# A new order for every queue of a fused attention and gated-convolution kernel, with 139 elementwise steps on another engine

## The chip, the cores and the metric

The kernel runs on one core of one Trainium2 chip. A core has TensorE (PE in the profile) for matrix products, three elementwise engines, VectorE (DVE), ScalarE (ACT) and GpSimd (POOL), and SyncE (SP), which here only issues DMAs. Each engine takes its instructions strictly from its own list; engines wait for each other by semaphores. TensorE writes its products to PSUM, a small memory that VectorE and ScalarE read; everything else lies in SBUF. The metric is the time on the device in microseconds (us), the median of several runs. One further execution was taken with the hardware profiler; every row below is from it.

## The reference

Four batches, eight heads, 768 positions, head width 64, model width 512. Four of the eight heads are full causal ("retrieval"); the others see the first 4 positions and a window of 64. The attention's output, heads side by side, is the input of a gated long convolution.

```python
scores = scale * np.matmul(q, k.transpose(0, 1, 3, 2))
mask = np.where(retr[0, :, 0, 0, None, None], full_mask, stream_mask)
scores = np.where(mask[None, :, :, :], scores, -1000000000.0)
a = np.exp(scores - np.max(scores, axis=-1, keepdims=True))
attn = np.matmul(a / (np.sum(a, axis=-1, keepdims=True) + 1e-09), v)

proj = x @ w_proj
x1, x2, x3 = (proj[..., :D], proj[..., D:2 * D], proj[..., 2 * D:])
x2_conv = np.fft.irfft(np.fft.rfft(x2, n=S, axis=1) * H, n=S, axis=1)
y = x1 * x2_conv * x3
return (y @ w_out).astype(np.float32)
```

Here `x` is the attention's output with its heads side by side, and `H` the spectrum of `filter_fft` along the positions.

## The kernel before

A short opening issues the loads of q and k of the first two head pairs (k of pair 0, q of pair 0, k of pair 1, q of pair 1, in this order, on SyncE), makes a few constants and the first of three parts of a table of angles, and checks which heads are full. Then the function `patterned` does everything else. It defines 995 named steps, each a handful of instructions, and issues them in the order of a long string of words, `FAST`. That string is the whole schedule: since nothing reorders afterwards, the words that belong to one engine stand in that engine's list in the order of the string. A word is a step's name, with `@n` where the step opens one of four PSUM slots of two banks, and `/s`, `/v`, `/p` or `/d` where the engine may be chosen: ScalarE, VectorE, GpSimd or a DMA. Where a step needs another's result, or a buffer that another still reads, the program waits by a semaphore, and whatever is queued behind it on that engine waits too.

```python
    for word in FAST.split():
        name, _, slot = word.partition("@")
        name, _, eng = name.partition("/")
        now.update(slot=slot, engine=eng)
        ops[name]()
```

The steps, by the names that the text uses (n is one of 16 head pairs, b one of 4 batches):

- `lq`, `lk`, `lv`: loads of q, k, v of a pair. `cq`, `ck`, `cv` (from pair 8 on `cqk` for both): casts to bf16.
- `T`, `E`: transposes of q and k on TensorE and their eviction from PSUM; from pair 8 on `T` is a DMA transpose. `kx`, `ks`, `vx`, `vs`: small copies that put the first 4 positions beside the window's keys and values.
- `sc`, `sb`, `ex`, `mk`, `at`: score products, a bias added by a product with a table `btab`, exponentials on ScalarE, masks, product with v. `rec`, `nm`: the row sums' reciprocal and the division, from PSUM into `attn`.
- `fd`, `fe`, `fA`, `fS`, `fb`, `fr`: sums and differences of the attention's output that fold its 768 positions, ahead of the transform `W`, evicted by `We`.
- `angle`, `turns`, `wrap`, `size`, `sin`, `cos`: the table `G` of the transform, made by ScalarE's sine. `Gt`, `Ge`: its transpose. `lfilt`, `fold`, `F`, `H`: the filter's load, folding, transform and scaling.
- `X`, `Xe`, `pa`, `pb`, `pc`, `sw`: the projection of the spectrum, and its product with the filter's. `c`, `ce`, `cv` with three numbers: the inverse transform and the sum and difference of its halves. `x1`, `x3`, `xs`, `g`, `y`: the two gates. `tn`, `te`: transposes of the attention's output. `o`, `oe`, `st`: output product, eviction and store. `lw`, `lwo`: weight loads.
- `blank`: products of zeros whose result is not used, which keep TensorE at work.

The helper that carries most engine choices is at L1101 to L1110:

```python
    def ev(out, in_):
        if now["engine"] == "v":
            nc.vector.tensor_copy(out=out, in_=in_)
        elif now["engine"] == "p":
            nc.gpsimd.tensor_copy(out=out, in_=in_)
        elif now["engine"] == "d":
            nc.sync.dma_start(out=out, in_=in_)
        else:
            nc.scalar.copy(out=out, in_=in_)

    def two(out, a, b, op):
        (nc.gpsimd if now["engine"] == "p" else nc.vector).tensor_tensor(out, a, b, op)
```

The division `nm` has two forms: on VectorE one instruction for the whole pair, on ScalarE (`/s`) twelve, one for each block of 128 rows and head.

Of the kernel before, what the change touches and what calls it, by code (L numbers as in the profile page):

```python
# [144 lines left out]
at4.1@1 at4.0 rec4 nm4/v kx6/s vs5/s sc6.1@2 sc6.0@3 ex6.1 pb0.1/p ex6.0 cqk8/p T8 at5.1@0 at5.0 sc6.2@1 ex6.2 rec5
nm5/v fe5/v pa0.2/v T7.1@2 T7.0 E7.1/s pc0.1/v x10.0.1@3 E7.0/s x10.0.0 xs0.0/s x10.1.0@1 H2.4 kx7/v ks7/s mr6
mk6.2 x30.0.1@0 x30.0.0 g0.0 x10.1.1 sc7.1@2 fd5/v xs0.1/s ex7.1 fe4/p pb0.2/v pc0.2/v fA5/v mk7.1 pb0.0/v
x10.3.1@3 x10.3.0 lk9 lq9 lv7 sc7.2@0 sc6.4@1 pa0.0/v xs0.3/s ex6.4 lq10 ex7.2 mk7.2 x10.2.1@2 tn4@3 mk6.0 pc0.0/v
fS5/v mk6.1 fb5/p x10.2.0 c0.1.0@1 te4/s cv6/s xs0.2/s x30.2.0@0 vx6/p x30.2.1 vs6/s ce0.1/s lwo g0.2 sc7.0@3 ex7.0
# [10 lines left out]
o0.4.1 nm9/v fe9/v Xe1.2/s fd9/v oe0.5/s x31.0.0@3 fA9/v kx11/p sc10.2@0 ex10.2 pb1.1/v sc11.1@2 fS9/v sc11.2@1  # L160
ex11.2 lv11 x31.0.1 x11.3.1@0 g1.0 mk11.2 pa1.1/v mk10.2 mr10 x11.3.0 vx10/p ex11.1 mk11.1 cv11/s vx11/v xs1.3/s
fb8/v vs11/s X1.0.0@1 X1.0.1 Xe1.0/s at10.1@3 at10.0 st0.3 T12 fb9/p sc11.0@2 ex11.0 sc12.0@0 x11.2.0@1 fr8 x11.2.1
sw1.0 rec10 pc1.1/v nm10/v W8.0@2 ex12.0 sw1.1 pb1.2/v W8.1 st0.5 xs1.2/s x11.1.1@3 mk11.0 x11.1.0 We8/s fd10/v
xs1.1/s tn10@0 at11.1@1 at11.0 te10/s pa1.0/v lk13 tn9@2 te9/s fr9 W9.1@3 W9.0 x31.2.1@0 fe10/v rec11 nm11/v fe11/v
pa1.2/v sc12.4@2 sc12.1@1 x31.2.0 fA10/p pc1.2/v lq13 We9/s ex12.4 fd11/v x31.1.0@3 tn11@2 x31.1.1 ex12.1 g1.2
te11/s sc12.3@1 sc12.2@0 fS10/v x12.0.1@2 x12.0.0 ex12.2 sc12.5@0 g1.1 ex12.3 x32.0.1@3 xs2.0/s c1.1.0@1 lv12 lq14
lk14 fb10/v pb1.0/v pc1.0/v exp0 fr10 W10.1@2 ce1.1/s lq15 W10.0 We10/s ex12.5 x32.0.0 cqk14/s fA11/p fS11/v mk12.1
cqk13/v c1.1.1 fr11 fb11/v g2.0 c1.0.1@2 lv14 c1.0.0 cv1.1.0 lk15 cv14/s cv1.1.1 W11.0@0 W11.1 c1.3.0@3 We11/s
c1.3.1 mk12.2 ce1.0/v cv1.0.1 c1.2.1@1 cv1.0.0 mk12.0 c1.2.0 X2.0.1@0 ce1.3/s y1.1/p cv1.3.1 X2.0.0 y1.0/v cv1.3.0
X2.1.0@2 cv12/s T13 kx13/v ce1.2/s cv1.2.0 cv1.2.1 Xe2.0/s pa2.0/v ks13/p cqk15/s X2.1.1 sc13.0@3 sc13.2@1 ex13.2  # L170
pb2.0/v y1.3/v at12.1@0 vx14/d Xe2.1/s y1.2/v lv13 ex13.0 cv13/v T14 ks14/s at12.0 rec12 nm12/v kx14/s x31.3.1@1
T15 x31.3.0 o1.1.0@2 g1.3 fd12/v fe12/p vs13/d vx13/d fA12/v sc13.1@3 sc14.1@0 sc14.2@1 mk13.0 ex13.1 lv15 mk13.1
o1.1.1 o1.0.0 ex14.1 o1.0.1 mk13.2 X2.2.1@3 kx15/v oe1.1/s mk14.1 ex14.2 st1.1 X2.2.0 Xe2.2/s pa2.1/v at13.1@0
sw2.0 ks15/v pb2.1/v at13.0 rec13 sc14.0@2 ex14.0 sw2.1 sc15.2@1 x12.2.0@3 x12.2.1 xs2.2/s mk14.2 tn12 nm13/v
ex15.2 x32.2.1@2 x32.2.0 sc14.4@3 sc14.3@0 ex14.4 pc2.1/v cv15/s sc15.0@1 g2.2 pc2.0/v sc15.1@3 pa2.2/v o1.2.0@2
o1.3.0 o1.3.1 ex15.1 fS12/p ex15.0 fe13/p fb12/v fd13/p vs14/d o1.2.1 ex14.3 fr12 x12.1.1@3 x12.1.0 mk14.0 mr14
fA13/v mk15.0 at14.0@1 at14.1 pb2.2/v x32.1.0@0 oe1.3/s x12.3.0@2 xs2.1/s mk15.1 W12.0@3 x12.3.1 W12.1 rec14 nm14/v
vx15/s mk15.2 vs15/s at15.1@1 at15.0 xs2.3/s We12/s x32.1.1 pc2.2/v c2.0.1@2 tn13 c2.1.0@3 fS13/v c2.0.0 fr13
ce2.1/s fb13/p rec15 nm15/v g2.1 fe14/p fd15/v st1.3 fd14/p fS14/v W13.1@1 fA14/v fr14 W13.0 We13/s c2.1.1 fb14/p
cv2.1.0 cv2.1.1 ce2.0/s cv2.0.1 o1.5.0@0 o1.5.1 o1.4.0 cv2.0.0 o1.4.1 c2.3.0@1 fe15/p tn14 oe1.5/s st1.5 fA15/v  # L180
W14.0@3 W14.1 We14/s fS15/p fb15/v c2.3.1 fr15 c2.2.1@2 y2.0/v c2.2.0 y2.1/v W15.1@0 W15.0 ce2.3/s We15/s x32.3.1@3
ce2.2/s x32.3.0 cv2.3.0 cv2.3.1 y2.3/v g2.3 cv2.2.1 cv2.2.0 y2.2/v X3.1.0@0 X3.2.0@1 X3.2.1 Xe3.2/v sw3.0 X3.1.1
sw3.1 Xe3.1/s pa3.2/v o2.0.0@3 o2.0.1 o2.1.0 o2.1.1 pa3.1/v oe2.1/s pb3.1/p X3.0.0@2 o2.4.0@1 o2.4.1 tn15@0 te15/s
pb3.2/v X3.0.1 o2.5.0 o2.5.1 pc3.1/v x33.0.0@3 x13.0.1@0 st2.1 Xe3.0/s x13.1.0@2 pa3.0/v pc3.2/v x13.0.0 x13.1.1
# [1717 lines left out]
```

## Time and profile before

| what | value |
|---|---|
| median of 3 runs | 188.08 us (187.79 to 188.16) |
| profiled execution, its span from first to last instruction | 188.0 us |
| TensorE busy | 171.7 us, 91%, 1688 instructions |
| VectorE busy | 152.6 us, 81%, 301 instructions |
| ScalarE busy | 143.3 us, 76%, 191 instructions |
| GpSimd busy | 64.1 us, 34%, 96 instructions |
| DMA | 33.67 MB, mean 179 GB/s |
| mean granted TensorE clock | 0.997 |

The span of the profiled execution and the median of the runs agree within 0.1 us, so a time worked out from the span needs no correction that a run could tell. A busy time is the time in which an engine had an instruction in its datapath. The page of the profile also gives, for a group of equal instructions, their count, busy time, the mean of one, and the idle time of the engine just before them with what ended it.

### The profile page before, as it was taken

The numbers are of one execution on the slowest core, as the hardware profiler recorded it, in microseconds if no ns is written. First come the engines' busy times: TensorE is split into PE (matmuls) and PEld (weight loads), VectorE is DVE, ScalarE is ACT, GpSimd is POOL, SyncE is SP. The second block draws the span as 40 slices with busy tenths as digits, with TensorE's granted clock in tenths as the row PEclk, the third lists the DMA queues.
The fourth block names the chain that finished last, engine by engine and source line by source line (L and its number), as shares of the span: only waits on it lengthen the run. The fifth ranks groups of instructions, "written<-read, shape, count | busy, mean of one in ns | idle before, by whom it ended". The sixth has DMA issues, their size and how long they took to land.

```text
span 188.0 us, 4376 instructions
## 1 busy us (share of the span) xinstructions
PE 171.7 (91%) x1688; PEld 103.9 (55%) x1704; DVE 152.6 (81%) x301; ACT 143.3 (76%) x191; POOL 64.1 (34%) x96
## 2 busy tenths in 40 slices
PE   0889996989999999999999999999999999999960
PEld 0346773644585556565556656475567644565430
DVE  6559676968999998998799999999799996388720
ACT  6689995879997998987999999899895526613330
POOL 3368750992080094443210111311406405400200
PEclk9999999999999999999999999999999999999998
DMA  5999999699999899999899988688942205300363
GB/s 182 309 271 281 194 187 287 151 260 228 218 210 203 180 192 210 184 232 234 193 249 257 225 180 176 137 138 225 127 125 55 112 2 157 122 3 0 113 248 104
DMA packets 77695, 33.67 MB, mean 179 GB/s; under 512 B 66850, under 2 KB 74082, under 8 KB 77666
## 3 DMA queue, kind: packets, MB, share of 16 engines
q1 hardware_dynamic: 74576, 30.29, 70.4%
q0 software_dynamic: 2944, 2.88, 10.1%
q8 instruction: 15, 0.25, 0.6%
q10 hardware_dynamic: 146, 0.13, 0.2%
q14 instruction: 14, 0.11, 0.2%
HBM read 24.64 MB, written 6.29 MB: 165 GB/s over the span
## 4 chain that ended last, share of the span: by engine, by line
PE 65%; DVE 14%; DMA 7%; POOL 4%; ACT 3%; issue 2%; SPq 0%; POOLq 0%; DVEq 0%
PE f_x_ps L1695 18%; PE f_X_ps L1660 10%; PE f_out_ps L1758 8%; PE f_c_ps L1725 7%; PE f_sc L1492 6%; PE f_att L1556 6%; DMA qk_ahead<-in_q_dram 4%; DMA f_qk_f<-in_q_dram 3%; DVE f_attn L1573 2%; ACT f_pT L1511 2%; PE f_W_ps L1617 2%; DVE f_P L1110 2%; PE f_sc L1505 2%; DVE f_fo L1110 1%; DVE turns L1736 1%
## 5 line engine op out<-in xcount | busy, mean ns | idle before, releaser
L1511 ACT ACTIVATE f_pT<-f_sc 128x1024 bf16<-128x1024 f32 (+3 forms) x68 | 58.7, 918 | 3.7 <-PE f_sc L1492 3.2
L1695 PE MATMUL f_x_ps<-f_xT,f_wproj 128*128 128x384 bf16 x256 | 46.7, 326 | 0.4 <-DVE f_attn L1573 0.3
L1695 PEld LDWEIGHTS <-f_wproj 128*128 128x128 bf16 x256 | 23.9, 98 | 16.5 <-issue 1.6
L1660 PE MATMUL f_X_ps<-f_wproj,f_xh 128*128 128x512 bf16 x92 | 22.3, 379 | 0.2
L1758 PE MATMUL f_out_ps<-f_wout,f_gy 128*128 128x512 bf16 x86 | 21.7, 379 | 0.3
L1492 PE MATMUL f_sc<-f_qkT 64*128 64x128 bf16 (+3 forms) x248 | 20.3, 250 | 0.0
L1725 PE MATMUL f_c_ps<-f_Gi,f_P 128*128 128x384 bf16 x96 | 18.4, 326 | 0.2 <-DVE f_gy L1714 0.2
L1110 POOL TENSOR_TENSOR f_fo<-f_attn 128x384 bf16<-128x384 bf16 x13 | 12.3, 954 | 15.0 <-DVE f_attn L1573 14.8
L1736 DVE TENSOR_TENSOR turns<-angle,f_c_ps 128x384 bf16<-128x384 f32 x32 | 16.3, 548 | 1.3 <-PE f_c_ps L1725 0.8
L1556 PE MATMUL f_att<-f_v_aug,f_pT 128*128 128x65 bf16 x392 | 17.2, 193 | 0.0
L1556 PEld LDWEIGHTS <-f_pT 128*128 128x128 bf16 x472 | 16.0, 97 | 2.1 <-issue 0.4
L1107 ACT COPY f_o<-f_out_ps 128x1024 f32<-128x1024 f32 (+2 forms) x12 | 10.2, 854 | 8.7 <-PE f_out_ps L1758 7.8
L1573 DVE TENSOR_TENSOR f_attn<-f_att,f_rec 128x768 bf16<-128x768 f32 x16 | 15.3, 955 | 0.6
L1492 PEld LDWEIGHTS <-f_qkT 64*128 64x128 bf16 x248 | 10.6, 94 | 9.3 <-issue 7.0
L1660 PEld LDWEIGHTS <-f_xh 128*128 128x128 bf16 x96 | 9.0, 98 | 10.3 <-issue 0.7
L1107 ACT CAST f_xh<-f_W_ps 128x768 bf16<-128x768 f32 x13 | 10.5, 807 | 4.5 <-PE f_W_ps L1617 2.3
L1758 PEld LDWEIGHTS <-f_gy 128*128 128x128 bf16 x92 | 8.6, 98 | 9.3 <-DVE f_gy L1718 0.3
L1107 ACT CAST f_X<-f_X_ps 128x1024 bf16<-128x1024 f32 x10 | 10.2, 1016 | 4.6 <-PE f_X_ps L1660 4.5
L1531 DVE TENSOR_TENSOR f_pT<-f_pT,mtab 128x1024 bf16<-128x1024 bf16 (+1 forms) x18 | 12.1, 688 | 1.4 <-ACT f_pT L1511 1.4
L1447 PE MATMUL f_qkT_ps<-identity,f_qk_bf 128*128 128x128 bf16 x96 | 7.9, 225 | 5.6 <-DVE f_qk_bf L1101 5.2
L1725 PEld LDWEIGHTS <-f_P 128*128 128x128 bf16 x96 | 9.0, 98 | 6.5 <-issue 0.6
L1110 POOL TENSOR_TENSOR f_br<-f_fo,f_uv 128x256 bf16<-128x256 bf16 x6 | 4.6, 765 | 21.3 <-DVE f_uv L1110 12.3
(132 smaller groups left out, 329.9 us busy)
## 6 DMA issues: line engine op xcount, KB each, us to landing
f_v_f<-in_v_dram SPq DMA_DIRECT2D x32, 192.0 KB, 4.4
out_dram<-f_o SPq DMA_DIRECT2D x17, 256.0 KB, 2.3
qk_ahead<-in_k_dram SPq DMA_DIRECT2D x6, 384.0 KB, 6.3
qk_ahead<-in_q_dram SPq DMA_DIRECT2D x6, 384.0 KB, 6.3
qk_ahead<-in_k_dram SPq DMA_DIRECT2D x10, 192.0 KB, 4.3
qk_ahead<-in_q_dram SPq DMA_DIRECT2D x10, 192.0 KB, 4.9
f_wproj<-in_moe_w_proj_dram POOLq DMA_DIRECT2D x6, 256.0 KB, 7.2
out_dram<-f_o SPq DMA_DIRECT2D x3, 512.0 KB, 4.4
```

The costliest lines, as they stand in the source:

```text
L1107: nc.scalar.copy(out=out, in_=in_)
L1110: (nc.gpsimd if now["engine"] == "p" else nc.vector).tensor_tensor(out, a, b, op)
L1492: nc.tensor.matmul(sc[:, bank, col:col + 128 * cnt], lhsT=keys, rhs=qkT(n)[rows, 0, 128 * i:128 * (i + cnt)], start=(col == 0 or not biase ...
L1511: nc.scalar.activation(out=pT(n)[:, c, :, 0:w], in_=held[f"sc.{n}.{c}"][:, :, 0:w], func=AF.Exp, scale=SCALE)
L1531: nc.vector.tensor_mul(some, some, near(c)[:, None].to_broadcast([128, 2, cols, 128]))
L1556: nc.tensor.matmul(att[:, hh, 65 * i:65 * i + 65], lhsT=pT(n)[:, c, bank, col:col + 128], rhs=values, start=(z == 0), stop=(z == len(here) ...
L1573: nc.vector.tensor_mul(attn(n).rearrange("p i hh d -> p hh i d"), rows[:, :, :, 0:64], held[f"rec.{n}"][:, :, :, None].to_broadcast([128, ...
L1660: nc.tensor.matmul(ps[:, u, :], lhsT=xh(b)[:, cc, chain, 128 * part:128 * part + 128], rhs=wproj()[:, cc, DM:2 * DM], start=(cc == 0), sto ...
L1695: nc.tensor.matmul(ps[:, s, 0:HS], lhsT=wproj()[:, cc, part * DM + cb * 128:part * DM + (cb + 1) * 128], rhs=xT(b)[:, cc, s * HS:s * HS + HS],
L1725: nc.tensor.matmul(ps[:, r, 0:HS], lhsT=P(b)[:, t, u, ch], rhs=Gi()[:, tile_no], start=(m == 0), stop=(m == 2))
L1736: fn(conv[:, half * HS:half * HS + HS], held[f"evs.{b}.{cb}"], held[f"c_ps.{b}.{cb}"][:, 1, 0:HS])
L1758: nc.tensor.matmul(ps[:, i % 2, :], lhsT=gy(b)[:, cb, i * 128:(i + 1) * 128], rhs=wout()[:, cb, :], start=(cb == 0), stop=(cb == NC - 1))
```

## The change

The string `FAST` is written anew. The same 995 steps stand in it, in another order, and 139 of them name another engine. No instruction's shape changes but where the engine has its own form (`nm` on ScalarE). The opening's steps are as before.

```diff
 FAST = """
-angle1 turns1 angle2 ck1/p cq0/p turns2 lq2 ones0 ck0/v wrap1 T0.1@0 wrap2 blank0@1 wrap0 sin2 size E0.1/s sin1 lk2
-cq2/p kz2 cos2 cq1/s T0.0 E0.0/v lv1 lk3 lv0 T1.0@2 ones2 cos1 T2.0@3 E2.0/v sc0.3@1 E1.0/s T1.1 mtab2 E1.1/s
...
+cq1/s lv0 cq0/v angle2 turns1 T1.0@0 turns2 angle1 wrap0 ck0/s lq2 wrap1 wrap2 T0.0@1 T0.1 blank0@2 size ck1/s E0.0/v
+E0.1/v E1.0/v mtab2 mtab3 kz1 cos1 ones1 T1.1 cos2 btab lv1 lk2 ones0 sc0.2@3 E1.1/v sc0.3@1 lq3 sin1 sin2 sc0.1@2
...
```

By engine the 139 steps go like this. To GpSimd 55: 39 from VectorE (`fd` 5, `fe` 3, `fA` 4, `fS` 5, `fb` 3, `y` 4, `pa` 2, `pc` 2, casts 6, small copies 5), 13 from ScalarE (`cqk` 3, `cv` 5, small copies 5) and 3 small copies from a DMA. From GpSimd 30: 24 to VectorE (casts 7, folds 9, `pb` 2, `y` 1, small copies 5) and 6 to ScalarE. From VectorE to ScalarE 26, among them `nm5`, `nm14` and `nm15`; from ScalarE to VectorE 27, among them `E` 7, `ce` 4 and `te` 3; one small copy goes from a DMA to ScalarE.

Two places show the new order. The first is ScalarE's list in the opening, from its first steps in `patterned` to the first exponential (`f_pT<-f_sc`). `qk_ahead_68` is the buffer of pair 1's q and k, `qk_ahead_65` that of pair 0; `f_G` is the table of sines and cosines; an `ACT_TABLE_LOAD` stands where ScalarE goes over from sine to exponential. Before:

```order
L1192 ACTIVATE turns<-fcol,tfrac 128x384 x2
L1214 ACTIVATE f_G<-angle 128x3x2x64
L1107 COPY f_qkT_3005<-f_qkT_ps_2983 128x768
L1214 ACTIVATE f_G<-angle 128x3x2x128
L1214 ACTIVATE f_G<-f_size,quarter 128x3x2x64
L1107 CAST f_qk_bf_2972<-qk_ahead_68 128x768
L1214 ACTIVATE f_G<-f_size,quarter 128x3x2x128
L1107 COPY f_qkT_3051<-f_qkT_ps_3029 128x768 x2
L1511 ACT_TABLE_LOAD
L1511 ACTIVATE f_pT_3076<-f_sc_3_3048 128x2x384
```

After, on the same engine and at the same place:

```order
L1106 CAST f_qk_bf_2969<-qk_ahead_68 128x768
L1191 ACTIVATE turns<-fcol,tfrac 128x384 x2
L1106 CAST f_qk_bf_2974<-qk_ahead_65 128x768
L1106 CAST f_qk_bf_2969<-qk_ahead_68 128x768
L1213 ACTIVATE f_G<-f_size,quarter 128x3x2x128
L1213 ACTIVATE f_G<-f_size,quarter 128x3x2x64
L1213 ACTIVATE f_G<-angle 128x3x2x128
L1213 ACTIVATE f_G<-angle 128x3x2x64
L1510 ACT_TABLE_LOAD
L1510 ACTIVATE f_pT_3088<-f_sc_3_3053 128x2x384
```

The cast of pair 1's q (`cq1`) has moved from behind most of the table to the head of the list, the casts of both k (`ck0`, `ck1`) have come over from the other engines, and the three evictions (`COPY f_qkT`) have gone to VectorE. On TensorE the transposes follow in the order `T1.0`, `T0.0`, `T0.1`, eight blanks, `T1.1`, where it was `T0.1`, eight blanks, `T0.0`, `T1.0`, `T2.0`. (In the changed file every line behind the string has a number smaller by one.)

The second place is GpSimd's list, from its first step in `patterned` to the load of the filter (`f_filt`). `mtab` is the table of masks from which `btab` is made. Before:

```order
L1103 CAST f_qk_bf_2972<-qk_ahead_68 128x768
L1103 CAST f_qk_bf_2974<-qk_ahead_65 128x768
L1383 MEMSET f_v_aug_2979 128x12
L1103 CAST f_qk_bf_3009<-f_qk_f_2_2977 128x768
...
L1165 AFFINE_SELECT mtab<-mtab 128x3x128
...
L1103 COPY f_v_x_3100<-f_v_aug_3078 64x520
L1227 TENSOR_SCALAR f_G<-par 128x3
L1103 CAST f_v_aug_3036<-f_v_f_2_3089 128x12x64
L1103 COPY f_v_x_3164<-f_v_aug_3036 64x4x65
L1264 DMA f_filt<-in_moe_filter_fft_dram 128x6x512
```

After:

```order
L1164 AFFINE_SELECT mtab<-mtab 128x3x128
...
L1102 CAST f_v_aug_3047<-f_v_f_0_2971 128x12x64
L1226 TENSOR_SCALAR f_G<-par 128x3
L1102 CAST f_qk_bf_3091<-f_qk_f_2_2989 128x768
L1378 MEMSET f_kx_3135 128x4x64
L1102 COPY f_v_x_3140<-f_v_aug_3032 64x520
L1102 CAST f_qk_bf_3164<-qk_ahead_65 128x768
L1263 DMA f_filt<-in_moe_filter_fft_dram 128x6x512
```

The mask table has moved ahead of all casts, the three casts of q and k of pairs 0 to 2 have left, and ahead of the filter's load now stand a write into the table `G` (the step `alt`), the casts of k of pairs 2 and 3, and a copy of pair 1's v that waits for its cast (`cv1`) on VectorE.

The third place is SyncE's list of loads, behind the load of v of pair 3 (`f_v_f_3`). The buffers `qk_ahead_68` and `qk_ahead_65` take the loads of pairs 4 and 6 here, `f_qk_f_8` those of pair 8. Before:

```order
L1401 DMA f_qk_f_5_3156<-in_k_dram 128x2x384
L1404 DMA f_qk_f_8_3302<-in_k_dram 128x6x64 x2
L1401 DMA qk_ahead_68<-in_k_dram 128x2x384
L1401 DMA qk_ahead_68<-in_q_dram 128x2x384
L1401 DMA qk_ahead_65<-in_q_dram 128x2x384
```

After:

```order
L1422 DMA f_v_f_2_3167<-in_v_dram 128x6x64 x2
L1400 DMA f_qk_f_5_3230<-in_k_dram 128x2x384
L1400 DMA f_qk_f_5_3230<-in_q_dram 128x2x384
L1400 DMA qk_ahead_68<-in_k_dram 128x2x384
L1400 DMA qk_ahead_68<-in_q_dram 128x2x384
L1422 DMA f_v_f_5_3474<-in_v_dram 128x6x64 x2
```

The load of pair 8's k, whose buffer must first be free of pair 5's k, no longer stands ahead of the loads of pair 4.

More of the change, by code (lines that the diff above doesn't have):

```diff
@@ L145 @@
[L145 to L149, printed above, removed]
@@ L160 @@
[L160 to L164, printed above, removed]
@@ L165 @@
[L165 to L184, printed above, removed]
@@ new lines @@
+We11/s y1.0/v c1.2.1 c1.3.1 X2.1.1@3 T14 cv1.3.0 ks13/s X2.0.1@1 X2.1.0 kx13/s cv1.3.1 y1.3/v ce1.2/v X2.0.0 at12.0@0
+Xe2.1/s st0.5 at12.1 sc13.0@3 lv15 cv1.2.1 cv1.2.0 kx14/v Xe2.0/s sc13.2@2 x31.3.0@1 rec12 ks14/p pa2.0/v nm12/v
+fd12/v ex13.2 x31.3.1 fe12/v cv14/p ex13.0 y1.2/p sc14.2@2 ex14.2 g1.3 tn12 sc13.1@0 o1.0.0@3 mk13.2 ex13.1 fS12/p
+o1.1.0 fA12/p o1.1.1 sc14.1@2 sc14.0@1 mk13.0 ex14.1 X2.2.0@0 o1.0.1 X2.2.1 cv15/v mk13.1 mk14.2 T15 ex14.0 vx13/p
+at13.0@2 vx15/v at13.1 vs14/s mr14 mk14.1 x12.2.0@1 x12.2.1 oe1.1/s kx15/p rec13 ks15/s nm13/v x32.2.0@3 Xe2.2/s
```

82 lines of the change are left out of this document (53 added, 29 removed).

## The prediction

> **What bounds the kernel now.** I read the page's busy times first, then four stretches of the span, then TensorE's waits, then the opening row by row.
>
> ```profile
> span 188.0 us, 4376 instructions
> PE 171.7 (91%) x1688; PEld 103.9 (55%) x1704; DVE 152.6 (81%) x301; ACT 143.3 (76%) x191; POOL 64.1 (34%) x96
> ```
>
> ```profile
> core 0: us, PE busy (x) PEld busy (x) DVE busy (x) ACT busy (x) POOL busy (x), PEclk, DMA share, GB/s
> 0.00:14.00 14.00, 7.92 (x50) 3.95 (x52) 8.38 (x27) 9.86 (x14) 6.61 (x23) 1.00 0.92 254
> 14.00:45.00 31.00, 28.29 (x378) 18.30 (x380) 23.67 (x40) 26.59 (x35) 19.11 (x31) 1.00 1.00 229
> 45.00:181.00 136.00, 134.93 (x1260) 81.36 (x1269) 120.14 (x237) 106.12 (x143) 38.35 (x43) 1.00 0.78 162
> 181.00:188.00 7.00, 0.60 (x6) 0.29 (x3) 0.42 (x1) 0.77 (x2) 0.00 (x0) 0.91 0.42 149
> ```
>
> TensorE bounds the kernel. It idles 14.00 − 7.92 = 6.08 us in the opening, 2.71 from 14 to 45, 1.07 from 45 to 181, and 6.40 at the end: 16.3 us in all. The change takes no product away, so the time after is these 171.7 us plus the idle time after. Relieving VectorE or GpSimd is worth at most what they cost TensorE in waits, 2.71 + 1.07 us outside the two ends. The profiled span (188.0) and the median (188.08) agree, so the sum on the span is the forecast for the median.
>
> ```profile
> PE f_qkT_ps L1447 <- DVE f_qk_bf L1101: 5.2, 1, 5.2
> PE f_F_ps L1293 <- DVE f_fold L1285: 1.4, 1, 1.4
> PE f_sc L1492 <- POOL f_kx L1103: 0.6, 1, 0.6
> ```
>
> These are TensorE's three largest waits (sum, count, longest). The first is the opening: nothing to transpose until VectorE has cast pair 0's k. The other two make up most of the 2.71 us.
>
> **The opening, the largest term.** TensorE and ScalarE in the first 16 us:
>
> ```profile
> 5.22 0.80 PE L1447 MATMUL f_qkT_ps<-identity,f_qk_bf 128*128 128x128 bf16 x6 [5.22 <-DVE f_qk_bf L1101]
> 5.81 3.60 PE L1143 MATMUL f_blank_ps<-blank 128*128 128x512 bf16 x8
> 9.32 0.94 PE L1447 MATMUL f_qkT_ps<-identity,f_qk_bf 128*128 128x128 bf16 x12
> 11.73 1.46 PE L1143 MATMUL f_blank_ps<-blank 128*128 128x512 bf16 x6
> 13.65 0.27 PE L1505 MATMUL f_sc<-f_btab,identity 128*128 128x128 bf16 x2 [0.46 <-DVE f_btab L1187]
> ```
>
> ```profile
> 3.78 1.12 ACT L1192 ACTIVATE turns<-fcol,tfrac 128x384 int32<-128x384 f32 x2 [0.41 <-DVE par L987]
> 6.53 0.52 ACT L1214 ACTIVATE f_G<-angle 128x384 bf16<-128x384 f32 x1 [1.63 <-DVE angle L1201]
> 7.64 0.84 ACT L1214 ACTIVATE f_G<-angle 128x768 bf16<-128x768 f32 x1
> 8.38 0.60 ACT L1214 ACTIVATE f_G<-f_size,quarter 128x384 bf16<-128x384 f32 x1
> 8.89 0.82 ACT L1107 CAST f_qk_bf<-qk_ahead 128x768 bf16<-128x768 f32 x1
> 9.61 0.93 ACT L1214 ACTIVATE f_G<-f_size,quarter 128x768 bf16<-128x768 f32 x1
> 12.75 1.28 ACT L1511 ACT_TABLE_LOAD   x1
> 14.04 2.64 ACT L1511 ACTIVATE f_pT<-f_sc 128x768 bf16<-128x768 f32 x3
> ```
>
> After, TensorE's first step is the transpose of pair 1's q (`T1.0`), and ScalarE's first is the cast it needs (`cq1/s`). Pair 1's q is the last of the opening's four loads:
>
> ```profile
> 2.33 0.47 SPq L1846 DMA_DIRECT2D qk_ahead<-in_q_dram  x1
> ```
>
> ```profile
> qk_ahead<-in_q_dram SPq DMA_DIRECT2D x6, 384.0 KB, 6.3
> ```
>
> ```profile
> 7.68 1.59 POOL L1103 CAST f_qk_bf<-qk_ahead 128x768 bf16<-128x768 f32 x2 [5.14 <-DMA qk_ahead<-in_k_dram]
> ```
>
> Issued at 2.33 with a median of 6.3 us to landing, it lands near 8.6. From below: GpSimd's cast at 7.68 had waited 5.14 us for a k load, pair 1's, which is ahead in the same queue. From above: ScalarE's cast of this very q started at 8.89 and the row shows no wait. I take 8.6, nearest to the issue's own row. With the cast's 0.82 us and a semaphore's 0.1 (my allowance), TensorE starts at 9.5 (8.5 to 9.8) and not at 5.22.
>
> Behind the waiting cast on ScalarE's list stand `turns1` and `turns2` (at 3.78 before), then `ck0/s` and `ck1/s`. So the cast of pair 0's k ends at 8.6 + 0.82 + 1.12 + 0.82 = 11.4, while `T1.0` and `T0.0` are done about 10.7 (two times about 0.6 us, between the rows' 0.80 for the first six and half of the 0.94 for twelve later ones): 0.6 us of idle time before `T0.1`. VectorE's `wrap` steps and the table of angles hang on `turns`; they come late too, and with them `btab` on VectorE's list. ScalarE needs, from 8.6, the sum 0.82 + 1.12 + 0.82 + 0.82 + (0.93 + 0.60 + 0.84 + 0.52) + 1.28 = 7.75 us until its first exponential: 16.3 instead of 14.04. TensorE meanwhile has `T0.1` (0.8), eight blanks (3.60), `T1.1` and the first scores, up to about 16; I allow 0.7 us of waiting for `btab` or the exponentials (0 to 2). Opening idle: 9.5 + 0.6 + 0.7 = 10.8 against 6.08, **+4.7 us** (+2.8 to +6.3).
>
> The blanks may run quicker. Eight took 3.60 us (450 ns each) right behind TensorE's first work, six took 1.46 (243 ns) later. After, three groups of transposes precede the eight, so some may run at the later rate: at most 8 × 0.207 = 1.7 us, but TensorE stands 0.6 us among them. **−0.5 us** (−0.9 to 0).
>
> The Trainium skill, page "TensorE: Matmul & The Clock Gate", section "What's actually happening", says that the array runs at half its clock until it has been busy for some 3.4 us. The two rows of blanks agree with it (450 against 243 ns). By that rule only some two of the eight blanks would be quick, as an estimate −0.4 us in place of −0.5.
>
> **The middle, 14 to 45.** Two waits stood there. The first is the filter:
>
> ```profile
> 18.91 1.04 POOL L1264 DMA_DIRECT2D f_filt<-in_moe_filter_fft_dram  x1
> 32.52 0.83 POOL L1103 CAST f_qk_bf<-qk_ahead 128x768 bf16<-128x768 f32 x1 [6.51 <-DMA qk_ahead<-in_k_dram]
> ```
>
> ```profile
> f_filt<-in_moe_filter_fft_dram POOLq DMA_DIRECT2D x1, 768.0 KB, 11.1
> ```
>
> It landed at 18.91 + 11.1 = 30.0, and the fold and TensorE waited 1.4 us. After, the load stands on GpSimd behind `alt`, two casts, a memset and the copy that waits for `cv1` on VectorE. Those start later with the opening, so I put the issue at 22 (18.9 to 25) and the landing at 33. The first product that needs it, `F2.0`, stands at about 36 in the new order, by the products ahead of it at before's durations. So this wait falls to 0 (up to +1.5 when the issue slips to 25 or GpSimd's list slips further).
>
> The second wait comes from GpSimd's stand of 6.51 us ahead of 32.52 for pair 4's load; the small copy `kx` (0.6 us of TensorE's time) stood behind it. That load was held up on SyncE's list by the load of pair 8's k:
>
> ```profile
> 24.41 0.96 SPq L1404 DMA_DIRECT2D f_qk_f<-in_k_dram  x2
> 26.53 3.20 SPq L1401 DMA_DIRECT2D qk_ahead<-in_q_dram  x2
> ```
>
> After, pair 8's no longer stands there, so SyncE issues pair 4's loads as soon as its buffer is free, and the wait goes. What stays of the 2.71 us is about 0.7, and I add 0.5 for the denser GpSimd list (19.1 of 31 us busy already): 1.2, **−1.5 us** (−2.5 to +0.8). The DMA share is 1.00 from 14 to 45, so what comes earlier for pair 4 comes later for another load; the 0.5 is for that too.
>
> **The late part, 45 to 181.** Counting the moved steps, VectorE has 39 + 26 fewer and 24 + 27 more, net 14 fewer; GpSimd has net 25 more, ScalarE net 7 fewer, the DMA queues 4 fewer. Most are of the kind of these rows:
>
> ```profile
> L1110 DVE TENSOR_TENSOR f_fo<-f_attn 128x384 bf16<-128x384 bf16 x19 | 7.3, 395 | 0.2
> L1110 POOL TENSOR_TENSOR f_fo<-f_attn 128x384 bf16<-128x384 bf16 x13 | 12.3, 954 | 15.0 <-DVE f_attn L1573 14.8
> L1573 DVE TENSOR_TENSOR f_attn<-f_att,f_rec 128x768 bf16<-128x768 f32 x16 | 15.3, 955 | 0.6
> L1107 ACT COPY f_kx<-f_qkT 128x16 bf16<-128x16 bf16 x2 | 0.5, 251 | 0.0
> ```
>
> VectorE is relieved of about 14 × 0.395 = 5.5 us and GpSimd gets 25 × 0.954 = 24 us. The three divisions on ScalarE are 12 instructions each; the shape is not in the trace, the nearest is a small copy at 251 ns, so 3.0 us each in place of 0.955 on VectorE. `nm5/s` lies where ScalarE runs exponentials for the next pairs; the pair's products behind it wait up to 2 us more. None of this takes anything from TensorE but waits, and only 1.07 us is there to take. Against it stands what GpSimd's work does to VectorE's. Two rows of one moment:
>
> ```profile
> 56.01 1.06 DVE L1110 TENSOR_TENSOR f_fo<-f_attn 128x384 bf16<-128x384 bf16 x1
> ```
>
> ```profile
> 55.95 0.90 POOL L1110 TENSOR_TENSOR f_fo<-f_attn 128x384 bf16<-128x384 bf16 x1
> ```
>
> VectorE's fold took 1.06 us instead of the mean 0.395 while GpSimd did the same kind of work: 0.66 us lost. If each of the net 25 steps cost VectorE that once, it would be 16.5 us against 5.5 us of relief, 11 us more work on an engine with 136.00 − 120.14 = 15.9 us free in this stretch. None of it blocked gives a stretch as before or, at best, no wait (−1.07). I take **+1.0 us** (−1.0 to +6), the idle time doubled, since most of these 11 us would fit in VectorE's free time, and nearest to the row of this stretch.
>
> The Trainium skill, page "SBUF — State Buffer", section "Who interferes with whom", says that VectorE and GpSimd share one pair of ports as an exclusive lock, that a VectorE instruction with two SBUF inputs contends with a GpSimd one that reads SBUF, and that one with at most one SBUF input, outside the two-port modes, does not. The two rows at 56 us agree: two SBUF inputs, 0.66 us lost. By that rule GpSimd work placed wholly beside VectorE's PSUM work would cost nothing, the late term would be 0, and the sum 190.7 in place of 191.7; and against it VectorE's casts and copies of SBUF data would be blocked too.
>
> The end (6.40 us idle) keeps its order of evict and store: 0 (±0.4).
>
> **The sum:** 188.0 + 4.7 − 0.5 − 1.5 + 1.0 = **191.7 us**.
>
> **The rivals.**
> *GpSimd blocks VectorE (slower still).* The 11 us of net blocked time fall where VectorE's evictions hold TensorE's PSUM slots. For it: VectorE is 88% busy from 45 to 181, and GpSimd's share nearly doubles there. Against: GpSimd idles 14.8 us before the folds waiting for `attn`, so many steps have slack. Half of the 11 us on TensorE's path gives 191.7 − 1.0 + 5.5 = 196.2; range 194 to 200.
>
> *Not slower.* The place is 14 to 181: the new order removes every wait of TensorE there (−3.78) and the opening costs its least (start at 8.5, no further idle but 0.4, +2.8, blanks −0.9): 186.1 at the very best, about 187.5 with half of one term missing. It decides when TensorE's idle time outside the 6.40 at the end is under 9.9 us, the 6.08 + 2.71 + 1.07 of before. For it: the causes of both large waits are indeed moved. Against: a start at 9.5 alone takes 9.5 of these 9.9 us.
>
> *It doesn't matter when TensorE starts.* If other chains set the stretch to 45 us anyway, the late start would be hidden: 188.0 − 1.5 + 1.0 = 187.5. Against it: TensorE is 28.29 of 31 us busy from 14 on; no room hides 4 us. This falls together with the case above.
>
> **How the numbers follow.** A change of 0.2% (0.4 us) is about what a measurement of this kernel can tell from none. The forecast, 189.5 to 194: 0.65. GpSimd blocks VectorE, 194 to 200: 0.20. Not slower, under 188.4: 0.10. Between 188.4 and 189.5: 0.05. Range: 188.9 to 196.5 leaves out about 0.12 below and 0.08 above. Faster by over 0.2%: 0.05; within: 0.05; slower: 0.90. The predicted time is the forecast's.
>
> **What the profile after would show.** Right: TensorE's first transpose near 9.5, waiting for a ScalarE cast that waits for `in_q_dram`; the first exponential near 16.3; no wait on `f_fold` or `f_kx` above 0.5 us; 1 to 3 us idle from 45 to 181; GpSimd busy about 90 us. The first rival shows as VectorE's folds and masks with longer means and TensorE waiting on VectorE for several us. Wrong: a first transpose before 8 (the loads land earlier than I read), or the filter late again with TensorE waiting at `F` for over 2 us, which the row 18.91 would then have as 25 or later.

## The result, and the profile after

The changed kernel takes 217.58 us (median of 4 runs, 215.66 to 218.84), 188.12 before: a ratio of 1.153, interval 1.144 to 1.162. The profiled execution has a span of 216.9 us. The page of after, its busy times:

```profile
span 216.9 us, 4421 instructions
PE 179.1 (83%) x1687; PEld 106.6 (49%) x1704; DVE 173.9 (80%) x287; ACT 143.9 (66%) x217; POOL 102.0 (47%) x121
```

The same stretches as before, with the last one up to the new end:

```profile
core 0: us, PE busy (x) PEld busy (x) DVE busy (x) ACT busy (x) POOL busy (x), PEclk, DMA share, GB/s
0.00:14.00 14.00, 3.95 (x23) 2.61 (x24) 8.55 (x24) 6.53 (x10) 5.50 (x20) 1.00 0.90 252
14.00:45.00 31.00, 27.47 (x370) 18.17 (x371) 23.31 (x41) 25.65 (x34) 18.90 (x28) 1.00 0.94 201
45.00:181.00 136.00, 117.35 (x1134) 69.68 (x1144) 120.39 (x195) 99.45 (x156) 67.24 (x68) 0.96 0.73 148
181.00:216.90 35.90, 30.34 (x166) 16.13 (x166) 21.67 (x30) 12.32 (x19) 10.40 (x5) 0.95 0.28 98
```

TensorE's idle time by stretch: 10.05 us (6.08 before), 3.53 (2.71), 18.65 (1.07) and 5.56 (6.40). So the 28.9 us are +4.0, +0.8, +17.6 and −0.8 of idle time, and +7.4 of busy time for the same products. The loss lies behind 45 us.

VectorE was to lose some 5.5 us of work. It is busy 21.3 us longer, with 14 instructions fewer (less the excess defined below, its work is 9.4 us shorter: 138.3 against 147.7). Its groups by shape, before (count, then busy us and mean ns):

```profile
L1736 DVE TENSOR_TENSOR turns<-angle,f_c_ps 128x384 bf16<-128x384 f32 x32 | 16.3, 548 | 1.3 <-PE f_c_ps L1725 0.8
L1110 DVE TENSOR_TENSOR f_P<-f_X,f_HAB 128x1024 bf16<-128x1024 bf16 x12 | 8.2, 686 | 1.0 <-ACT f_X L1107 0.8
L1601 DVE SCALAR_TENSOR_TENSOR f_br<-f_uv,f_fo 128x256 bf16<-128x256 bf16 x11 | 5.1, 468 | 0.1
L1543 DVE TENSOR_TENSOR f_pT<-f_pT,mtab 128x768 bf16<-128x768 bf16 x3 | 1.7, 550 | 0.0
```

and after:

```profile
L1735 DVE TENSOR_TENSOR turns<-angle,f_c_ps 128x384 bf16<-128x384 f32 x32 | 16.4, 547 | 6.3 <-PE f_c_ps L1724 3.6 <-ACT angle L1106 2.6
L1600 DVE SCALAR_TENSOR_TENSOR f_br<-f_uv,f_fo 128x256 bf16<-128x256 bf16 x11 | 9.5, 876 | 0.8 <-POOL f_uv L1109 0.6
L1109 DVE TENSOR_TENSOR f_P<-f_X,f_HAB 128x1024 bf16<-128x1024 bf16 x10 | 8.8, 889 | 0.5 <-ACT f_X L1106 0.5
L1542 DVE TENSOR_TENSOR f_pT<-f_pT,mtab 128x768 bf16<-128x768 bf16 x3 | 3.8, 1266 | 0.0
```

What reads PSUM (`f_c_ps`) takes what it took. What reads two tiles in SBUF takes 1.3 to 2.3 times as long in the rows shown; other such shapes hardly changed (the 128x384 folds `f_fo`: a mean of 395 ns before, 418 after). Summed over all VectorE instructions that are over 0.05 us above the shortest of the same name and shape (in that trace or in before's), the time above it is 4.9 us before and 35.6 after; "excess" below is this sum. (Against the shortest of its own trace alone it is 4.4 and 32.4, the figures in some expectations.)

One place shows how it reaches TensorE. VectorE, GpSimd and TensorE of after around 76 us, each from its timeline:

```profile
73.61 1.15 DVE L1100 CAST f_qk_bf<-f_qk_f 128x1536 bf16<-128x1536 f32 x1
74.69 1.68 DVE L1600 SCALAR_TENSOR_TENSOR f_br<-f_uv,f_fo 128x256 bf16<-128x256 bf16 x1
76.29 2.45 DVE L1542 TENSOR_TENSOR f_pT<-f_pT,mtab 128x768 bf16<-128x768 bf16 x1
78.66 0.68 DVE L1530 TENSOR_TENSOR f_pT<-f_pT,mtab 128x1024 bf16<-128x1024 bf16 x1
79.26 0.94 DVE L1713 TENSOR_TENSOR f_gy<-angle,f_x_ps 128x768 bf16<-128x768 bf16 x1
```

```profile
74.01 2.07 POOL L1102 CAST f_qk_bf<-qk_ahead 128x1536 bf16<-128x1536 f32 x1
76.04 0.80 POOL L1276 DMA_DIRECT2D f_wout<-in_moe_w_out_dram  x1
76.84 1.48 POOL L1102 CAST f_qk_bf<-qk_ahead 128x1536 bf16<-128x1536 f32 x1
```

```profile
75.83 0.81 PE L1724 MATMUL f_c_ps<-f_Gi,f_P 128*128 128x384 bf16 x4
80.25 0.41 PE L1491 MATMUL f_sc<-f_qkT 64*128 64x128 bf16 x6 [3.62 <-DVE f_gy L1713]
```

VectorE's fold and mask (means of 0.47 and 0.55 us before) lasted 1.68 and 2.45 us beside GpSimd's two casts, and each ended 0.3 to 0.4 us after the end of the cast beside it. (The mask's record begins 0.55 us ahead of the second cast's; the profile doesn't show when one began to hold the other.) The product `g0.2`, which frees the PSUM slot of the next scores, stood behind them; TensorE waited 3.62 us. Then it pays again:

```profile
80.00:85.00 5.00, 4.75 (x48) 3.10 (x48) 4.53 (x10) 2.88 (x5) 1.50 (x1) 0.66 1.23 227
134.00:139.00 5.00, 5.00 (x25) 3.03 (x25) 2.85 (x6) 2.17 (x2) 1.02 (x2) 0.66 1.11 255
172.00:178.00 6.00, 5.16 (x28) 2.97 (x28) 2.25 (x7) 3.49 (x8) 2.00 (x3) 0.72 0.29 108
```

In these three windows of after the mean granted clock (third number from the end) is 0.66, 0.66 and 0.72, each behind a wait (3.62 us to 80.25, 2.9 to 134, and 1.1 and 1.6 us close together before 173). Within each window the clock is at 0.50 for 3.41 us (from 80.39, 135.01 and 172.55) and at 1.00 for the rest. 5 × 0.34 + 5 × 0.34 + 6 × 0.28 = 5.1 us of the 7.4 us of longer busy time is this; the other 2.3 us stay open.

### The profile page after: what moved, and what is told of

Read it like the earlier page. It is cut to its first block, busy times and chain, and to the rows that moved or that the text cites. A ratio compares the mean times of both kernels' runs of the same rounds, so it can differ in the third digit from the quotient of the medians.

```text
span 216.9 us, 4421 instructions
## 1 busy us (share of the span) xinstructions
PE 179.1 (83%) x1687; PEld 106.6 (49%) x1704; DVE 173.9 (80%) x287; ACT 143.9 (66%) x217; POOL 102.0 (47%) x121
## 5 line engine op out<-in xcount | busy, mean ns | idle before, releaser
L1491 PE MATMUL f_sc<-f_qkT 64*128 64x128 bf16 (+3 forms) x248 | 21.1, 251 | 9.5 <-DVE f_gy L1713 6.5
L1724 PE MATMUL f_c_ps<-f_Gi,f_P 128*128 128x384 bf16 x96 | 21.7, 361 | 7.5 <-DVE angle L1100 4.0
L1109 POOL TENSOR_TENSOR f_fo<-f_attn 128x384 bf16<-128x384 bf16 x17 | 18.3, 1082 | 15.4 <-DVE f_attn L1572 7.8
L1757 PE MATMUL f_out_ps<-f_wout,f_gy 128*128 128x512 bf16 x86 | 23.2, 382 | 0.4
L1106 ACT COPY f_o<-f_out_ps 128x1024 f32<-128x1024 f32 (+2 forms) x14 | 11.7, 852 | 9.5 <-PE f_out_ps L1757 7.5
L1724 PEld LDWEIGHTS <-f_P 128*128 128x128 bf16 x96 | 9.8, 106 | 15.7 <-issue 11.2
L1530 DVE TENSOR_TENSOR f_pT<-f_pT,mtab 128x1024 bf16<-128x1024 bf16 (+1 forms) x18 | 15.6, 882 | 1.3 <-ACT f_pT L1510 1.2
L1109 POOL TENSOR_TENSOR f_uv<-f_fo 128x256 bf16<-128x256 bf16 x11 | 9.1, 835 | 15.7 <-DVE f_fo L1109 8.1
L1106 ACT CAST f_xh<-f_W_ps 128x768 bf16<-128x768 f32 x15 | 11.6, 800 | 7.1 <-PE f_W_ps L1612 6.6
L1100 DVE COPY f_qkT<-f_qkT_ps 128x768 bf16<-128x768 bf16 x10 | 9.4, 954 | 5.7 <-PE f_qkT_ps L1446 3.2
L1102 POOL CAST f_qk_bf<-qk_ahead 128x768 bf16<-128x768 f32 (+1 forms) x8 | 9.4, 1176 | 8.7 <-DMA qk_ahead<-in_q_dram 8.6
```

The costliest lines, as they stand in the source:

```text
L1491: nc.tensor.matmul(sc[:, bank, col:col + 128 * cnt], lhsT=keys, rhs=qkT(n)[rows, 0, 128 * i:128 * (i + cnt)], start=(col == 0 or not biase ...
L1530: nc.vector.tensor_mul(some, some, near(c)[:, None].to_broadcast([128, 2, cols, 128]))
L1724: nc.tensor.matmul(ps[:, r, 0:HS], lhsT=P(b)[:, t, u, ch], rhs=Gi()[:, tile_no], start=(m == 0), stop=(m == 2))
L1757: nc.tensor.matmul(ps[:, i % 2, :], lhsT=gy(b)[:, cb, i * 128:(i + 1) * 128], rhs=wout()[:, cb, :], start=(cb == 0), stop=(cb == NC - 1))
```

## The experiments

Theory A: the late loss is VectorE blocked by GpSimd. Theory B: it is the new order, whoever does the small steps. The first three kernels part order and engines.

**Order alone.** After, with every step on before's engine.

```diff
-cq1/s lv0 cq0/v ... ck0/s ... ck1/s ... nm5/s ... cqk9/p ...
+cq1/s lv0 cq0/p ... ck0/v ... ck1/p ... nm5/v ... cqk9/s ...
```

> The order of after, with each of the 139 steps on the engine it had before. Theory A (the late loss is VectorE blocked by GpSimd's added work: VectorE's excess over the shortest instruction of each form is 32.4 us after against 4.4 before): the blocking falls to under 10 us, and the time to 193 to 198, the opening's 4 us and a little. Theory B (the late loss is the new order itself: waits of one engine's list for another, whoever does the small steps): it stays above 210.

222.1 us (ratio 1.181, 1.169 to 1.194): slower than after itself, with an excess of 16.0 us, and GpSimd busy 68 us. Theory A as stated falls.

**Engines alone.** Before, with every step on after's engine.

```diff
-... ck1/p cq0/p ... ck0/v ... cq1/s ... nm5/v ... cqk9/s ...
+... ck1/s cq0/v ... ck0/s ... cq1/s ... nm5/s ... cqk9/p ...
```

> The order of before, with each of the 139 steps on the engine it has after. Theory A: GpSimd's extra 30 to 38 us of work block VectorE in the old order too, VectorE's excess comes to 20 us or more, and the time to 200 to 215. Theory B: 188 to 194, since the order is that of before.

229.7 us (1.220, 1.210 to 1.231), excess 26.4. Theory B falls too: on before's own order the moved steps cost 41 us. Order and engines were each made for the other.

**Only the 55 steps back that came onto GpSimd.**

```diff
-... cqk9/p ... fA5/p ... fS10/p ...
+... cqk9/s ... fA5/v ... fS10/v ...
```

> After, with only the 55 steps that came onto GpSimd put back on their former engines (the other 84 stay moved). Theory A: close to e1_order_only, 193 to 200, although VectorE is then given 39 steps more; VectorE's excess under 10 us. Theory B: above 210, more than after since VectorE and ScalarE have more to do.

213.1 us (1.133, 1.124 to 1.141), excess 17.6, with VectorE given 39 steps. Only 4.5 us come back: theory A's 193 to 200 and theory B's "more than after" both fail. TensorE's clock stays at 1.00 from 45 to 181 us and its busy time falls by 2.5 us to 176.6; its idle time in that stretch is still 15.7 us.

**The opening, mended.** After with its first 18 words re-ordered, and `ck0` on VectorE.

```diff
-cq1/s lv0 cq0/v angle2 turns1 T1.0@0 turns2 angle1 wrap0 ck0/s lq2 wrap1 wrap2 T0.0@1 T0.1 blank0@2 size ck1/s
+turns1 angle1 turns2 ck0/v angle2 cq0/v lv0 lq2 wrap0 T0.1@1 blank0@2 wrap1 wrap2 T0.0 ck1/s cq1/s T1.0@0 size
```

> After, with its first 18 words in another order and ck0 on VectorE, so that pair 0's k is cast and transposed first and pair 1's q last. TensorE starts near 5.2 instead of 9.81. If the late start is carried to the end (the prediction's reading), the time falls by 3.5 to 4.5 us, to 213 to 214; if later waits hide it, it stays within 1 us of 217.

216.3 us (1.148, 1.141 to 1.156): 1.3 us less, which the overlapping intervals don't tell from after, although TensorE starts at 5.26. Of the 4.5 us, 2.35 are lost at once (`T1.1` waits for an eviction), and the wait at `g0.2` stays, with a longer stretch of slow clock behind it. So most of what is won early is given back.

**GpSimd without reads.** After, with GpSimd as busy, reading almost nothing: each of its steps works on two elements of a row (`few`) and then writes zeros over the result, so the kernel leaves out these steps' values.

```diff
         elif now["engine"] == "p":
-            nc.gpsimd.tensor_copy(out=out, in_=in_)
+            nc.gpsimd.tensor_copy(out=out[few], in_=in_[few])
+            nc.gpsimd.memset(out, 0.0)
...
-        (nc.gpsimd if now["engine"] == "p" else nc.vector).tensor_tensor(out, a, b, op)
+        if now["engine"] == "p":
+            nc.gpsimd.tensor_tensor(out[few], a[few], b[few], op)
+            nc.gpsimd.memset(out, 0.0)
+            nc.gpsimd.memset(out, 0.0)
+        else:
+            nc.vector.tensor_tensor(out, a, b, op)
```

> After, with GpSimd's folds, products, casts and copies replaced by an operation of the same kind on two elements of each row, which waits for the same data, and writes of zeros over the whole result that take about as long (two for a fold or product, one for a cast or copy); the values are left out. GpSimd stays about as busy and as late, but reads almost nothing. Theory A (GpSimd's reads block VectorE, and this is the late loss): VectorE's excess falls from 35 us to under 10, TensorE's idle time behind 45 us (17.5) to under 6, the time to 193 to 200. Theory C, formed after e1_order_only (222) and e2_engines_only (229.7): the order of each list fits only the durations it was made with, and blocking is one of several ways in which steps come late; then the time falls by 5 to 12 us, to 206 to 213, and waits for ScalarE's evictions stay.

201.5 us (1.066, 1.060 to 1.072): 16.1 us less than after. The page and the late stretch of this kernel:

```profile
PE 171.9 (86%) x1687; PEld 104.1 (52%) x1704; DVE 145.6 (73%) x287; ACT 142.7 (71%) x217; POOL 108.9 (54%) x258
```

```profile
45.00:181.00 136.00, 127.10 (x1217) 75.90 (x1223) 106.81 (x209) 103.70 (x164) 80.01 (x183) 1.00 0.78 153
```

With GpSimd busier than ever (108.9 us), VectorE does the work of after in 145.6 us, 28.3 less; the excess is 5.9, the late idle time 8.9 instead of 18.65, and the clock is 1.00. TensorE's busy time is that of before. So reads by GpSimd make up 16 of the 29 us; between the two profiled executions it is 17, 10 of idle time and 7 of clock and stretched products. Both forecasts miss: theory A's 200 by 1.5 us and its 6 us of idle time, theory C's 206 by more. Blocking is the larger part and not all. The replacement takes away both directions, GpSimd's hold on VectorE and VectorE's on GpSimd (the cast of 2.07 us at 74.01 took 1.48 at 76.84); the runs don't part these two.

**The price of a read, by itself.** Before with 40 extra GpSimd instructions where it idled: sums that read, or writes of zeros.

```diff
+    spare = sb.tile([128, 2, 3, 64], BF16, name="f_spare")
+    nc.vector.memset(spare, 0.0)
+    EXTRA = {'lw2.0': 2, 'fe4': 4, 'cqk10': 1, ...}
...
         ops[name]()
+        for _ in range(EXTRA.get(name, 0)):
+            nc.gpsimd.tensor_tensor(spare, spare, spare, ALU.add)
```

> Before, with 40 extra sums on GpSimd of the fold's shape (128x384), on a spare tile and for nothing, put where GpSimd idled behind 46 us: some 38 us of GpSimd work, as much as after has more than before, with no step delayed by its own queue. Theory A: VectorE's excess rises by 10 us or more, and the time to 195 to 205. Theory C: the excess rises as much, and so does the time, to above 192, since the order has no slack. If blocking is hidden by VectorE's idle time: under 190.

> As e8_reads_added, with two writes of zeros in place of each extra sum: GpSimd about as busy, without reads. If reading is what blocks VectorE, the time is that of before within 1 us (187.5 to 189) and VectorE's excess stays near 5 us; if any GpSimd work does, it is that of e8_reads_added.

With reads 198.6 us (1.050, 1.041 to 1.059), excess 21.9; with writes 189.1 (1.002, 0.999 to 1.005), excess 6.8. The pages, reads first, then writes:

```profile
PE 174.1 (89%) x1688; PEld 105.0 (54%) x1704; DVE 168.5 (86%) x302; ACT 144.3 (74%) x191; POOL 102.2 (52%) x136
```

```profile
PE 171.9 (92%) x1688; PEld 104.4 (56%) x1704; DVE 153.7 (82%) x302; ACT 143.6 (76%) x191; POOL 98.7 (53%) x176
```

VectorE's busy time grows by 15.9 us for 38 us of reading, 0.42 us each microsecond, and by 1.1 for 35 us of writing; the time by 10 us and by nothing. In before the 64 us of GpSimd work that were there stand beside 4.9 us of excess, 0.08 each. The price depends on what VectorE does at that moment, as a count over the traces bears out. Of GpSimd's work that reads, before has 33.0 us beside VectorE instructions that use PSUM and 8.9 us beside those that read two tiles in SBUF; after has 22.7 and 49.0; the order alone, on before's engines, 16.8 and 22.2. The excess (4.9, 35.6, 16.0) follows the second number, though a stretched instruction also lengthens its own overlap. The Trainium skill, page "SBUF — State Buffer", section "Who interferes with whom", says that a VectorE instruction with two SBUF inputs contends with a GpSimd instruction that reads SBUF, not with one that only writes it; the two runs agree, with 15.9 against 1.1 us.

**Two casts.** The place at 76 us alone.

```diff
-... tn5@0 cqk10/p lv8 ... T10 cqk9/p nm6/v ...
+... tn5@0 cqk10/s lv8 ... T10 cqk9/s nm6/v ...
```

> After, with the two casts cqk9 and cqk10 (1.5 us each alone; in after they lie beside fr5, mr6 and mk7, which took 1.26, 1.85 and 0.6 us longer than their shortest) on ScalarE instead of GpSimd. By the blocking, TensorE's wait of 3.62 us for g0.2 falls under 1.5 us, the slow clock behind it (2.4 us of longer products between 75 and 90 us) goes, and the time falls by 3 to 6 us. If it is only a matter of the order on VectorE's list, the wait stays above 2.5 us and the time within 1.5 us of 217.6.

214.7 us (1.138, 1.129 to 1.147). The wait at `g0.2` falls from 3.62 to 0.45 us and the clock stays at 1.00 up to 90 us: the mechanism at this place. The time falls by 2.9 us (the interval just touches after's), a little under the expected 3 to 6, since two waits for ScalarE follow (0.8 us for `We5`, 1.2 for `ex8.4`), which now has the casts.

**The first 45 us.** The two strings cut at word 236 and joined crosswise: once before's first 236 words with the rest from after, once the reverse.

```diff
-cq1/s lv0 cq0/v angle2 turns1 T1.0@0 ...
+angle1 turns1 angle2 ck1/p cq0/p turns2 ... (236 words of before, then what is left in after's order)
```

> The first 236 words of before (to about 45 us), then the remaining steps in the order and on the engines of after. It takes the opening's and the middle's loss away and keeps the late one. If the parts add up: 217.6 less 4.8 (idle time to 45 us: 13.6 after, 8.8 before), so 212 to 214. If after's late part is slow only because everything comes late or in another phase behind its own opening: under 200.

> The first 236 words of after (to about 45 us), then the remaining steps in the order and on the engines of before. If the opening's loss is carried to the end and nothing else comes with it: 188 + 4.8 = 192 to 194. If before's late part takes it up: under 190. If a shift between the lists wakes further waits there: above 196.

210.5 us (1.114, 1.103 to 1.124) for the first and 197.2 (1.046, 1.039 to 1.053) for the second. After's first 45 us cost 7 us ahead of after's late part, and 9 ahead of before's. Both are more than the 4.8 us of idle time that they contain; in the second, 2 us of idle time come behind 45 us (3.06 against 1.07). A kernel that comes 5 us late into a list made for another moment loses a little more.

**Both taken away.** The first of these two, without GpSimd's reads.

> e6_before_to_45 with GpSimd's reads left out as in e4_no_reads: the first 45 us of before, the late part of after without blocking. If the opening (7 us in e6_before_to_45) and the blocking (16 us in e4_no_reads) add up: 217.6 - 7 - 16 = 194 to 196, and 6 to 8 us are left for the late waits on other engines. If the two overlap: 197 to 201. If blocking and opening are all: 188 to 190.

198.9 us (1.054, 1.047 to 1.061): 2.6 less than without reads alone. The losses overlap, and some 10 us remain, 9 against the control below. This stretch of it:

```profile
45.00:181.00 136.00, 127.41 (x1222) 76.20 (x1222) 104.95 (x207) 100.94 (x162) 79.87 (x185) 1.00 0.74 146
```

TensorE idles 8.6 us there while VectorE is busy 77% and ScalarE 74%: no engine is full. The waits are many and short, 0.3 to 2.1 us, for casts and evictions on all three engines.

**The four pairs without blocking.** The same replacement in the order alone, in before, and in the engines alone.

> e1_order_only (222.1) with GpSimd's reads left out as in e4_no_reads: the order of after on the engines of before, without blocking. VectorE's excess was 16 us there, so if blocking costs here what it costs in after (16 us of time for 30 us of excess), 9 us go and 213 are left: then the order itself, on engines that it was not made for, is the larger part. If every wait of the late part came from blocking: 193 to 196.

> Before with GpSimd's reads left out in the same way, as the control of the replacement: VectorE's excess of 4.9 us goes, and since 1.07 us of waiting is all that TensorE has there, 186.5 to 188.5. Above 190, the replacement itself would cost time, and the price of blocking read from e4_no_reads would be too small.

> e2_engines_only (229.7) with GpSimd's reads left out: the order of before on the engines of after, without blocking. VectorE's excess was 26 us there; at the rate of after 14 us go and 216 are left. If blocking is all: 193 to 196. Together with e4, e13 and e14 this gives the four pairs of order and engines without blocking.

| order | engines | with reads | without reads | difference |
|---|---|---|---|---|
| before | before | 188.5 | 190.0 | −1.5 |
| after | before | 222.1 | 216.8 | 5.3 |
| before | after | 229.7 | 217.8 | 11.8 |
| after | after | 217.6 | 201.5 | 16.1 |

The control costs 1.5 us (1.009, 1.005 to 1.013) instead of nothing, since the two writes of some steps take longer than what they replace; the price of blocking is rather 17 to 18 than 16 us, if the replacement costs as much in after. In the order alone it is 5.3 us, where I expected 9. Without GpSimd's reads a crossed pair still loses 27 to 28 us. So the engines of after do fit its order; it is a schedule of its own, which without blocking would take 11.5 us more than the control.

**Two loads.** Before with after's better place for one or both.

```diff
-... sc1.2@0 cv0/p vx1/p ... vx2/p lfilt kx2/v ... Gt1@0 lk8 Ge1/v lk4 ... tn1@2 lq4 te0/v ...
+... sc1.2@0 lfilt cv0/p vx1/p ... vx2/p kx2/v ... Gt1@0 Ge1/v lk4 ... tn1@2 lq4 lk8 te0/v ...
```

> Before, with two loads moved and nothing else: the load of pair 8's k behind that of pair 4's q (as after has it), and the filter's load ahead of cv0 and vx1 on GpSimd. The two waits of 1.38 and 0.56 us between 14 and 45 us go, so 186.0 to 187.2 against 187.8, if the DMAs (share 1.00 there) only change places among loads that nobody waits for; 187.5 to 189 if the filter's 768 KB delay the loads of pairs 3 to 5.

> Before with only the load of pair 8's k moved behind that of pair 4's q. e11_loads lost time since the earlier filter delayed pair 5's k, for which GpSimd stood 4.2 us; without that move the wait of 0.56 us at kx goes: 0.3 to 0.7 us less than before on the same chip. No gain, if GpSimd then waits for another load as long.

Both loads: 192.5 us (1.014, 1.007 to 1.022), slower. The filter came 3.4 us earlier, and what came later was the k of pair 5: GpSimd stood 4.19 us for it, with the small copy for TensorE's scores behind it. Two rows of GpSimd's timeline, and TensorE's wait (sum, count, longest):

```profile
15.47 1.02 POOL L1264 DMA_DIRECT2D f_filt<-in_moe_filter_fft_dram  x1
27.13 1.59 POOL L1103 CAST f_qk_bf<-f_qk_f 128x768 bf16<-128x768 f32 x2 [4.19 <-DMA f_qk_f<-in_k_dram]
```

```profile
PE f_sc L1492 <- POOL f_kx L1103: 3.3, 1, 3.3
```

One load alone: 188.9 us (1.001, 0.997 to 1.005), no difference; the wait for `kx` is gone, that for the fold is 1.6 us instead of 1.4. No kernel here beats before.

## Why the prediction was wrong

**The opening held.** TensorE's first transpose stood at 9.81 (forecast 9.5), waiting for the cast of pair 1's q:

```profile
8.86 0.83 ACT L1106 CAST f_qk_bf<-qk_ahead 128x768 bf16<-128x768 f32 x1 [5.50 <-DMA qk_ahead<-in_q_dram]
9.81 1.44 PE L1446 MATMUL f_qkT_ps<-identity,f_qk_bf 128*128 128x128 bf16 x12 [9.81 <-ACT f_qk_bf L1106]
12.10 3.59 PE L1142 MATMUL f_blank_ps<-blank 128*128 128x512 bf16 x8
16.99 2.64 ACT L1510 ACTIVATE f_pT<-f_sc 128x768 bf16<-128x768 f32 x3 [0.34 <-PE f_sc L1504]
```

The first exponential came at 17.0 (16.3), the idle time rose by 4.0 us (4.7). The −0.5 for quicker blanks did not come: eight took 3.59 us, as before. Net 4.0 against 4.2.

**The middle held in its parts and failed in its sum.** The filter was issued at 21.53 (22), and the waits for the fold and for `kx` are gone. But 3.53 us of idle time stood there instead of 1.2: TensorE waited for ScalarE's evictions (0.89 us at `E3.1`, 1.34 at `We1`), which I had not traced through the new lists. +0.8 instead of −1.5. The two rows:

```profile
27.39 0.49 PE L1446 MATMUL f_qkT_ps<-identity,f_qk_bf 128*128 128x128 bf16 x6 [0.89 <-ACT f_qkT L1106]
44.22 0.23 PE L1491 MATMUL f_sc<-f_qkT 64*128 64x128 bf16 x2 [1.34 <-ACT f_xh L1106]
```

**The late part is the step that failed**, "I take +1.0 us (−1.0 to +6)": +17.6 us of idle time. The mechanism was named, as the first rival, at 194 to 200 and 0.20. Its size went wrong in three ways. First the count: I charged the net 25 added steps, 0.66 us each, 16.5 us. The runs show 28.3 us (173.9 − 145.6). Every GpSimd step counts that now stands beside VectorE work in SBUF: shared out by overlap, of the 32 us 18 or 19 go to the 55 new steps and 12 to 14 to steps that GpSimd had before, where the whole excess was 4.9. The low rate of before, 0.08 us for each microsecond, goes with where its 64 us stood: in the order alone the same steps on the same engines have an excess of 16.0 us. Second the cover: I let it fit into VectorE's 15.9 free us. Between 66 and 80 us VectorE is busy 13.86 of 14.00 (12.73 before) and TensorE 10.20 (13.78 before); a free microsecond elsewhere doesn't help a list that is worked through in order. Third the other lists: even without reads 8.9 us of idle time stay behind 45 us, where 1.07 had been. The sign named for the rival stands there: behind the opening TensorE's two largest waits (sum, count, longest) are for VectorE.

```profile
PE f_sc L1491 <- DVE f_gy L1713: 6.5, 3, 3.6
PE f_c_ps L1724 <- DVE angle L1100: 4.0, 2, 2.9
```

**TensorE's busy time was not a constant.** "The time after is these 171.7 us plus the idle time after" is wrong by 7.4 us, some 5 of them in the three windows where the mean clock was 0.66 to 0.72. None of them comes in the kernel without reads. No term of the sum had this, though the blanks of the opening show the same two rates.

**The other side.** "Not slower" never came near: TensorE's idle time outside the end is 32.2 us, where it was to be under 9.9. That the change would cost time was forecast for the opening, and by measure that is 4 of the 29 us.

What stays open: of the 11.5 us that after's own order and engines lose without blocking (201.5 against the control's 190.0), some 3 to 4 us are the opening (without reads, before's first 45 us against after's; the replacement itself adds 1.4 us of idle time to before's first 45). Which steps make the other 8 or so was not settled; no single wait of TensorE behind 45 us is over 2.1 us in either kernel.

## What to carry to other kernels

GpSimd's work has no price of its own: here a microsecond of it cost VectorE 0.08 us where the order had put it beside PSUM work, and 0.42 us put in where GpSimd idled, so count each step against what VectorE does at that moment, those that didn't move included. In this kernel, with TensorE 99% busy over a long stretch, order and engine assignment hold only together, and a forecast for a rewritten schedule must walk through the evictions on each list rather than add up loads. And a wait of TensorE of some 3 us can cost 1.7 us more, by 3.41 us at half the clock behind it.

## What was not expected of the hardware

- Beside a GpSimd cast a VectorE mask of 0.55 us lasted 2.45 us, until just behind the cast's own end; as much GpSimd time in writes did next to nothing (excess 6.8 us against 21.9 with reads).
- TensorE's clock fell to half for 3.41 us behind waits of 2.9 and 3.6 us, and behind two of 1.1 and 1.6 us. It didn't each time: the wait of 2.86 us stands in the kernel with two casts moved too, and as 2.87 us in the kernel with before's first 45 us, and neither has slow products behind it. The slow stretches of after start 16 and 11 times 3.41 us apart. In the 3.41 us ahead of each, TensorE was busy 0.14, 1.02 and 1.01 us; in the kernel with before's first 45 us a border of such steps parts the wait, and the emptier step has 1.39 us of work. So it seems to count where a wait falls; no run tests that, and no exact limit comes out (1.49 us was followed by slow clock with the two casts moved). The Trainium skill, page "TensorE: Matmul & The Clock Gate", section "What's actually happening", gives an idle window of about 3.4 us for it; here waits of 2.9 us sufficed.
- A division on ScalarE takes twelve instructions of 343 ns (median), which overlap: `nm5` took 2.6 us in all, where I had put 3.0.
